# One PV run per eight score units throughout, ten score buffers to the end, and a VectorE write between the two halves of a bank

## The chip, the cores and the metric

One of the eight cores of a Trainium2 chip runs the kernel. The metric is the device time of one execution in microseconds; the median of three runs counts.

## The reference

`x` is 2048 x 512. A 32-head attention (head width 16) and a gated feed-forward block are computed from the same `x` and mixed per row by a sigmoid gate. All is float32.

```
qkv = x @ wqkv;  scores = q k^T / 4;  p = softmax(scores);  a = concat(p v) @ wo
b = (silu(x @ w1) * (x @ w3)) @ w2          # w1, w3: 512 x 1792, w2: 1792 x 512
g = sigmoid(sum(x * gate_w));  out = g * a + (1 - g) * b
```

## The kernel before

**Head of the program.** `x` is transposed and split into a rounded high part and a rest. The first Q and K columns and all of V are projected. Then one long main stretch begins, and a short ending follows it.

**The main stretch** is written out by hand as a string of letters, `order`, that is walked once. TensorE executes its instructions in that order.

- `Q` is one *score unit* (`score`, matmul in L719, exponential in L723). For one head pair, 128 keys and 512 queries, two matmuls of 50 rows each run side by side in the two row halves of the array and fill one `S` tile (`psum2()`, two tiles in all). ScalarE's exponential of 128 x 1024 turns the tile into one score buffer `p0` to `p9`. There are 1024 units, 32 for each head pair and half of the queries.
- `P` stands for two units' PV products (`pv`, L706). Four matmuls write four column groups of the accumulator `acc`. After 32 units `evac` copies `acc` out on VectorE (L687) and stores it.
- `F` is one *work slot* (`feed`). Everything else is cut into 158 *blocks*, each an accumulation of 12 or 42 matmuls into one of three banks (`bank()`): the remaining Q and K projections and the gate and up products (L409), the down products (L518), and the first output products (L597). The upper 64 rows of the array run a whole block first; then the lower 64 rows run the same block with the other half of the contraction into the same bank. Upper and lower half work on different blocks side by side, one matmul each per slot. After the lower half, the block's `done` function takes the bank off on VectorE.

`state_f` holds the two blocks in work. `REST` is the number of slots between the end of a block and the reuse of its bank. `GAP` is how many score units must lie between the end of an upper half and the start of the lower half of the same block. Nothing else than the order on TensorE stands between the two halves.

`order` has two kinds of period, each with eight units:

```
one = "QFFF" * 7 + "QPPPP"
two = ["QFFF" * 5 + "QPPQQPP", "QFFF" * 6 + "PPQQPP"]
order = "QQFFF" + one * LONG + "".join(two[...] for i in range(short))
order += "QFFF" * 4 + "QPPQPP"
```

`LONG` is 83 and `short` 44; with `MID` = 0 only the first entry of `two` is used. At the last Q ahead of a P, the exponentials of the SiLU that are due (L437, list `soon`) are issued behind the unit's own. VectorE's small pieces of work (`small`: reciprocals in L440, the addition in L438, products in L458) are issued one or two at each Q, and so are loads and the stages of the softmax division (`divide`, `reciprocals`).

In the first 83 periods all ten score buffers are used. Later only eight come back (`if n < 8 or issued < WIDE`); `p8` and `p9` then hold two rows of blocks of `wo` (`load_wo`) and a pair of tiles in `divide`.

**The ending** finishes the last blocks (`while feed(0, 0)`), divides the last heads, and projects and mixes the last rows.

Of the kernel before, what the change touches and what calls it, by code (L numbers as in the profile page):

```python
# [8 lines left out]
F32 = mybir.dt.float32  # L9
F32R = mybir.dt.float32r  # L10
# [7 lines left out]
P = 128  # L18
S = 2048
D = 512  # L20
F = 1792
# [6 lines left out]
NPAIR = H // 2  # L28
# [5 lines left out]
def gated_mix_kernel(ctx: ExitStack, tc: tile.TileContext, x, wqkv, wo, w1, w3, w2, gate_w, out):  # L34
# [18 lines left out]
    nc = tc.nc  # L53
# [3 lines left out]
    const = ctx.enter_context(tc.tile_pool(name="const", bufs=1))  # L57
# [23 lines left out]
    def slot(tag, dtype=F32R, shape=(P, 512)):  # L81

        return (fw if tag[0] == "f" else fk).tile(list(shape), dtype, name=tag, bufs=BUFS.get(tag, 2))
# [4 lines left out]
    def bank():  # L88
        return psum.tile([P, 512], F32, name="f", bufs=3)
# [21 lines left out]
    xn, xH, xL = {}, {}, {}  # L111
# [282 lines left out]
    wk = ctx.enter_context(tc.tile_pool(name="wk", bufs=1))  # L394
# [10 lines left out]
    def w_product(chunk, which, b):  # L405
        def product(ps, r, n):
            w = chunk["w"][which]
            k, i = divmod(n, 3)
            nc.tensor.matmul(ps, w[i == 2][r, k, :], (xL if i == 1 else xH)[b][r, k, :],  # L409
                             start=n == 0 and r.start == 0, stop=n == 3 * ND - 1 and r.start > 0)  # L410
        return product

# [67 lines left out]
    w2H, w2L, hs, wo_, ot = [], [], {}, {}, {}  # L480
    SETS = (("raw", "raw", "raw", "gw", "fh1", "fl1", "fh3", "fl3"), ("fh1", "fl1", "fh3", "fl3", "fr", "fr", "fr", "hx"))

    def halves_of(src, hi, lo, tag):

        r = slot(tag, F32)
        n = hi.shape[-1]
        nc.sync.dma_start(r[:, 0:n] if len(src.shape) == 2 else r[:, 0:n].rearrange("p (f t) -> p f t", t=P), src)
        nc.gpsimd.tensor_copy(hi, r[:, 0:n])  # L488
        nc.gpsimd.tensor_sub(lo, r[:, 0:n], hi)  # L489
# [7 lines left out]
    def load_piece(t, q):  # L497
        hi, lo = (slot(SETS[t % 2][2 * q + i]) for i in range(2))
        tag = "fr" if t == 0 or t == 1 and q < 2 else "sg"
        n = min(4, NF - 4 * q)  # L500
        src = h_d[512 * q:512 * q + P * n, P * t:P * t + P].rearrange("(f p) t -> p f t", p=P)
        halves_of(src, hi[:, 0:P * n], lo[:, 0:P * n], tag)
        hs.setdefault(t, []).append((hi, lo))

    def load_wo(k):
        if k < 2:
            hi, lo = w2H[3][:, 2 + k, :], w2L[3][:, 2 + k, :]
        else:
            both = wk.tile([P, 2, 512], F32R, name=f"p{NP - k + 1}")
            hi, lo = both[:, 0, :], both[:, 1, :]  # L510
        halves_of(wo[P * k:P * k + P, :], hi, lo, "sg")
        wo_[k] = hi, lo

    def h_product(t):
        def product(ps, r, n):
            f, i = divmod(n, 3)
            q, o = divmod(f, 4)
            nc.tensor.matmul(ps, hs[t][q][i == 2][r, P * o:P * o + P], (w2L if i == 1 else w2H)[q][r, o, :],  # L518
                             start=n == 0 and r.start == 0, stop=n == 3 * NF - 1 and r.start > 0)
            if r.start and i == 2 and (o == 3 or f == NF - 1):  # L520
                if t + 2 < NT:
                    load_piece(t + 2, q)
                elif t == NT - 2:
                    load_ot(q)
                elif q < 2:
                    load_ot(4 + q)
        return product

    def h_done(t):
# [11 lines left out]
    def load_ot(t):  # L541
        n = (0, 1, 2, 3, 2, 3, 0, 1)[t]
        hi, lo = (slot(SETS[0][2 * n + i]) for i in range(2))
        halves_of(N_d[:, P * t:P * t + P].rearrange("(k p) t -> p k t", p=P), hi[:], lo[:], "fr" if t >= 4 else "sg")
        ot[t] = hi, lo
# [3 lines left out]
    def reciprocals(k, half):  # L549

        rows = lambda d: d[8 * k:8 * k + 8, 1024 * half:1024 * half + 1024].rearrange("h (a t) -> h a t", a=16)
        nc.sync.dma_start(dd, rows(D_d))
        for _ in range(5):
            yield
        nc.vector.reciprocal(dd, dd)
        yield
        nc.sync.dma_start(rows(R_d), dd)

    def fetch_o(k, b, o, r, e=nc.sync):
        e.dma_start(o, O_d[P * k:P * k + P, 512 * b:512 * b + 512])  # L560
        src = R_d[8 * k:8 * k + 8, 512 * b:512 * b + 512]
        nc.sync.dma_start(r, bass.AP(tensor=src.tensor, offset=src.offset, ap=[[S, 8], [0, DH], [1, 512]]))

    def divide(k, half):

        yield from reciprocals(k, half)
        for b in (2 * half, 2 * half + 1):
            for _ in range(5):
                yield
            if half == 0:  # L570
                o, r = slot("hx", F32), slot("gw", F32)
            else:
                both = wk.tile([P, 2, 512], F32, name=f"p{NP - 1}")
                o, r = both[:, 0, :], both[:, 1, :]
            fetch_o(k, b, o, r)
            for _ in range(7):
                yield
            nc.gpsimd.tensor_mul(o, o, r)
            for _ in range(3):
                yield  # L580
            nc.sync.dma_start(N_d[P * k:P * k + P, 512 * b:512 * b + 512], o)
            yield
        if (k, half) == (2, 1):
            load_wo(2)
# [3 lines left out]
    def load_bt(t, tag="gs"):  # L588
        bt[t] = slot(tag, F32)
        nc.sync.dma_start(bt[t], B_d[P * t:P * t + P, :])  # L590

    def o_product(t):
        def product(ps, r, n):
            if n == 0 and r.start:
                load_bt(t)
            k, i = divmod(n, 3)
            nc.tensor.matmul(ps, ot[t][i == 2][r, P * k:P * k + P], wo_[k][i == 1][r, :],  # L597
                             start=n == 0 and r.start == 0, stop=n == 3 * ND - 1 and r.start > 0)
        return product

# [47 lines left out]
    source = blocks()  # L648

    ready, state_f = [], dict(upper=None, lower=None, started=0, ended=0)  # L650
    REST, GAP = 7, 3
    left_at = []

    def feed(rest=REST, gap=GAP):

        st = state_f
        used = st["started"] - 3
        if st["upper"] is None and (used < 0 or used < st["ended"] and left_at[used] + rest <= clock):
            block = next(source, None)
            if block:  # L660
                st["upper"] = [*block, bank(), 0]
                st["started"] += 1
        if st["lower"] is None and ready and ready[0][0] + gap <= issued:
            st["lower"] = ready.pop(0)[1]
        did = 0
        for name, r in (("upper", slice(0, 64)), ("lower", slice(64, P))):
            t = st[name]
            if t is None:
                continue
            product, done, length, ps, n = t  # L670
            did += 1
            product(ps, r, n)
            t[4] = n + 1
            if n + 1 == length:
                st[name] = None
                if name == "upper":
                    t[4] = 0
                    ready.append((issued, t))
                else:
                    done(ps)  # L680
                    st["ended"] += 1
                    left_at.append(clock)
        return did
# [18 lines left out]
    def pv(two):  # L702
        for j, half, k, gq, n, p in two:
            for h in range(2):
                r = 32 * (2 * gq + h)
                nc.tensor.matmul(acc[r:r + DH + 1, :], V[:, k, 2 * j + h, :], p[:, h, :],  # L706
                                 start=k == 0, stop=k == NT - 1)
            if n < 8 or issued < WIDE:
                free.append(n)
        if k == NT - 1:  # L710
            evac(j, half)

# [15 lines left out]


    NP = 10  # L730
    PERIODS = 8 * NPAIR
    LONG, MID = 83, 0
    WIDE = 8 * LONG
    one = "QFFF" * 7 + "QPPPP"
    two = ["QFFF" * 5 + "QPPQQPP", "QFFF" * 6 + "PPQQPP"]
    short = PERIODS - 1 - LONG
    order = "QQFFF" + one * LONG + "".join(two[(i + 1) * MID // short > i * MID // short] for i in range(short))
    order += "QFFF" * 4 + "QPPQPP"
    free = list(range(NP))

    units = iter([(j, half, k, gq) for half in range(2) for j in range(NPAIR) for k in range(NT) for gq in range(2)])
    pend, issued, clock = [], 0, 0
# [26 lines left out]
            pend = pend[2:]  # L769
    assert not pend and issued == 64 * NPAIR  # L770

    assert state_f["upper"] is None and all(b[0] < issued for b in ready)
    for _ in reciprocals(ND - 1, 1):
        pass
    k = ND - 1
    orr = [(slot("fr", F32), slot("sg", F32)) for _ in range(2)]
    for b in (2, 3):
        fetch_o(k, b, *orr[b - 2], nc.scalar)
    while feed(0, 0):
        pass  # L780
    assert state_f["ended"] == NBLOCK and not small and not later and not stages and not soon and not loads


    for t in (NT // 2 - 2, NT // 2 - 1):
        ps = bank()
# [4 lines left out]
    for t in range(NT // 2, NT):  # L790
        n, r = divmod(t - NT // 2, 2)
        if n < 2:
            if r == 0:
                both = psum2()
# [17 lines left out]
    for b in (2, 3):  # L812
        o, r = orr[b - 2]
# [34 lines left out]
```

## Time and profile before

| | |
|---|---|
| runs | 1418.3, 1418.87, 1421.13 us; median 1418.87 |
| profiled execution: span (the only time that the page has of it) | 1417.6 us |
| TensorE matmul / weight load busy | 1408.8 us (99%) / 833.7 us (59%) |
| ScalarE busy | 1033.2 us (73%) |
| VectorE / GpSimd busy | 449.4 us (32%) / 321.1 us (23%) |
| DMA | 141.42 MB, mean 100 GB/s |

The page has the engines' busy shares, the span in 40 slices, the DMA queues, the chain of work that ended last, and the costliest groups of instructions (line, engine, tiles, count, busy time, mean of one, idle time ahead of it and what ended that). A timeline row has its start, its length, the instruction and, in brackets, the idle time before it with what ended it; `x2` means that two instructions in a row are merged. PE is TensorE, ACT ScalarE, DVE VectorE, POOL GpSimd, SP the engine that issues most DMAs.

### The profile page before, as it was taken

To read this page: it belongs to the slowest core of one execution; us is meant where nothing else is said; L and a number is where in the kernel's file an instruction comes from. 1 tells how busy PE (TensorE), PEld (TensorE's weight loads), DVE (VectorE), ACT (ScalarE), POOL (GpSimd) and SP (SyncE) were. 2 spreads that over 40 slices of the span, in tenths; PEclk is the share of its full clock that TensorE was granted. 3 is DMA by queue.
4 is the path that set the end of the run, shared out by engine and by line. 5 is a ranking of instruction groups with operands and counts; after the bars stand their busy time and mean duration, and the time that the engine had idled before them with its cause. 6 is when DMAs were issued, how large, how long until landed. Compare 5 with 4: busy or idle time off the path is not lost.

```text
span 1417.6 us, 28518 instructions
## 1 busy us (share of the span) xinstructions
PE 1408.8 (99%) x11399; PEld 833.7 (59%) x11399; DVE 449.4 (32%) x845; ACT 1033.2 (73%) x1153; POOL 321.1 (23%) x356
## 2 busy tenths in 40 slices
PE   9999999999999999999999999999999999999998
PEld 7865656656556566565565665655555555554556
DVE  4421102464555545455464545400000000000013
ACT  4556767777777777777777777777788778877870
POOL 5014443011011100110110015441332332233230
PEclk9999999999999999999999999999999999999999
DMA  7554455342124432223233234543534443345445
GB/s 197 141 121 114 126 140 128 73 110 69 46 61 85 113 69 61 70 72 87 68 76 79 76 81 122 136 101 74 126 81 102 104 105 70 66 112 106 106 133 182
DMA packets 112668, 141.42 MB, mean 100 GB/s; under 512 B 16400, under 2 KB 70672, under 8 KB 109456
## 3 DMA queue, kind: packets, MB, share of 16 engines
q1 hardware_dynamic: 110384, 135.72, 39.6%
q10 hardware_dynamic: 2144, 3.80, 0.8%
q8 instruction: 92, 1.51, 0.5%
q14 instruction: 48, 0.39, 0.1%
HBM read 90.70 MB, written 48.76 MB: 98 GB/s over the span
## 4 chain that ended last, share of the span: by engine, by line
PE 93%; POOL 0%; DMA 0%; DVE 0%; ACT 0%; issue 0%; SPq 0%; ACTq 0%; POOLq 0%
PE acc L706 32%; PE f L409 27%; PE S L719 19%; PE f L518 11%; PE f L597 1%; PE f L95 0%; PE f L97 0%; PE f L96 0%; DMA fr<-in_B_w_dram 0%; PE S L97 0%; PE S L96 0%; PE S L95 0%; POOL xL L489 0%; POOL fl L489 0%; DVE sg L458 0%; POOL xH L488 0%
## 5 line engine op out<-in xcount | busy, mean ns | idle before, releaser
L723 ACT ACTIVATE p<-S 128x1024 f32<-128x1024 f32 x1024 | 967.5, 1026 | 308.4 <-PE S L719 307.1
L706 PE MATMUL acc<-p,V 128*17 128x512 f32 x4096 | 473.5, 594 | 0.0
L719 PE MATMUL S<-Qt,Kt 50*128 50x512 f32 x2048 | 427.9, 413 | 1.1 <-POOLq L278 0.6
L719 PEld LDWEIGHTS S<-Qt,Kt 50*128 50x128 f32 x2048 | 193.8, 184 | 187.4 <-ACT p L723 80.4
L706 PEld LDWEIGHTS acc<-p,V 128*17 128x17 f32 x4096 | 102.8, 97 | 274.1 <-issue 273.9
L409 PE MATMUL f<-xL,fh 64*128 64x512 f32 x1024 | 205.1, 391 | 0.0
L409 PE MATMUL f<-xH,fl 64*128 64x512 f32 x1024 | 204.9, 390 | 0.0
L409 PE MATMUL f<-xH,fh 64*128 64x512 f32 x1024 | 204.7, 390 | 0.0
L440 DVE RECIPROCAL sg<-sg 128x64 f32<-128x64 f32 x448 | 201.2, 509 | 1.9
L409 PEld LDWEIGHTS f<-xL,fh 64*128 64x128 f32 x1024 | 99.4, 187 | 21.2
L409 PEld LDWEIGHTS f<-xH,fl 64*128 64x128 f32 x1024 | 98.5, 185 | 20.1
L409 PEld LDWEIGHTS f<-xH,fh 64*128 64x128 f32 x1024 | 99.4, 187 | 17.7
L321 POOL CAST fh<-fr 128x512 fp32r<-128x512 f32 x32 | 21.6, 674 | 371.1 <-DMA fr<-in_B_w_dram 246.5
L687 DVE COPY u<-acc 128x512 f32<-128x512 f32 x32 | 22.1, 692 | 257.0 <-PE acc L706 257.0
L518 PE MATMUL f<-xH,fl 64*128 64x512 f32 x224 | 82.2, 391 | 0.5 <-POOL fl L489 0.5
L518 PE MATMUL f<-xL,fh 64*128 64x512 f32 x224 | 82.2, 391 | 0.3 <-POOL xL L489 0.3
L518 PE MATMUL f<-xH,fh 64*128 64x512 f32 x224 | 82.1, 391 | 0.0
L518 PE MATMUL f<-xH,raw 64*128 64x512 f32 x192 | 74.9, 390 | 0.0
L532 DVE TENSOR_SCALAR gs<-f,omg 128x512 f32<-128x512 f32 x16 | 12.0, 751 | 176.4 <-PE f L518 176.4
L432 DVE COPY gs<-f 128x512 f32<-128x512 f32 x56 | 38.7, 691 | 78.1 <-PE f L409 78.1
L518 PE MATMUL f<-xH,fr 64*128 64x512 f32 x160 | 62.4, 390 | 0.0
L454 DVE TENSOR_TENSOR raw<-f,gs 128x512 f32<-128x512 f32 x50 | 34.1, 682 | 82.7 <-PE f L409 82.7
(216 smaller groups left out, 1309.6 us busy)
## 6 DMA issues: line engine op xcount, KB each, us to landing
Kt<-kH_d SPq DMA_DIRECT2D x128, 128.0 KB
h_d<-sg SPq DMA_DIRECT2D x56, 256.0 KB
sg<-h_d SPq DMA_DIRECT2D x43, 256.0 KB
fr<-in_B_w_dram SPq DMA_DIRECT2D x42, 256.0 KB
Qt<-qH_d SPq DMA_DIRECT2D x128, 64.0 KB
Kt<-kL_d SPq DMA_DIRECT2D x64, 128.0 KB
fr<-in_A_wqkv_dram SPq DMA_DIRECT2D x18, 256.0 KB
Qt<-qL_d SPq DMA_DIRECT2D x64, 64.0 KB
```

What stands on the lines that cost most here:

```text
L321: nc.gpsimd.tensor_copy(wh, r)
L409: nc.tensor.matmul(ps, w[i == 2][r, k, :], (xL if i == 1 else xH)[b][r, k, :], start=n == 0 and r.start == 0, stop=n == 3 * ND - 1 and r.s ...
L432: nc.vector.tensor_copy(gs, ps)
L440: small.append(lambda q=q: nc.vector.reciprocal(sg[:, q:q + 64], sg[:, q:q + 64]))
L454: nc.vector.tensor_mul(gu, ps, st["gs"])
L518: nc.tensor.matmul(ps, hs[t][q][i == 2][r, P * o:P * o + P], (w2L if i == 1 else w2H)[q][r, o, :], start=n == 0 and r.start == 0, stop=n = ...
L532: nc.vector.tensor_scalar(y, ps, omg[:, t:t + 1], None, op0=OP.mult)
L597: nc.tensor.matmul(ps, ot[t][i == 2][r, P * k:P * k + P], wo_[k][i == 1][r, :], start=n == 0 and r.start == 0, stop=n == 3 * ND - 1 and r. ...
L687: nc.vector.tensor_copy(u, acc)
L706: nc.tensor.matmul(acc[r:r + DH + 1, :], V[:, k, 2 * j + h, :], p[:, h, :], start=k == 0, stop=k == NT - 1)
L719: nc.tensor.matmul(ps[:, h, :], Kt[i][r:r + 50, P * k:P * k + P], Qt[i][r:r + 50, t:t + 512], start=True, stop=True)
L723: nc.scalar.activation(p, ps, AF.Exp, scale=SCALE)
```

## The change

All periods become alike: two units, then the work slots, then units spread among slots, and one PV run of eight units. The work slots, 2403 over 127 periods, are shared out evenly (18 or 19 in each); the string's head and tail stay. All ten score buffers stay in use, and the two parts of `wo` and the tiles of `divide` get tiles of their own; the scratch for dynamic DMA descriptors is made smaller, which gives the room. When an upper half ends, VectorE writes one element (`tick`) after its last matmul, and the first matmul of the lower half waits for that write. `REST` and `GAP` are 9 and 6 and both count slots; a lower half may start earlier where no upper half is in work.

```diff
-            both = wk.tile([P, 2, 512], F32R, name=f"p{NP - k + 1}")
+            both = wk.tile([P, 2, 512], F32R, name=f"wo{k}")
...
-                both = wk.tile([P, 2, 512], F32, name=f"p{NP - 1}")
+                both = wk.tile([P, 2, 512], F32, name="od")
...
-    REST, GAP = 7, 3
+    REST, GAP = 9, 6
+    tick = const.tile([1, 1], F32, name="tick")
+    def after(ins, earlier):
+        tc.add_manual_dep(ins.ins, earlier.ins.name, ...)
...
-        if st["lower"] is None and ready and ready[0][0] + gap <= issued:
+        if st["lower"] is None and ready and (ready[0][0] + gap <= clock or st["upper"] is None):
...
-            product(ps, r, n)
+            ins = product(ps, r, n)
+            if turn and n == 0:
+                after(ins, turn)
...
-                    t[4] = 0
-                    ready.append((issued, t))
+                    t[4], t[5] = 0, nc.vector.memset(tick, 0.0)
+                    after(t[5], ins)
+                    ready.append((clock, t))
...
-            if n < 8 or issued < WIDE:
-                free.append(n)
+            free.append(n)
...
-    PERIODS = 8 * NPAIR
-    LONG, MID = 83, 0
-    WIDE = 8 * LONG
-    one = "QFFF" * 7 + "QPPPP"
-    two = ["QFFF" * 5 + "QPPQQPP", "QFFF" * 6 + "PPQQPP"]
-    ...
+    PERIODS = 8 * NPAIR - 1
+    PRODUCTS = 2403
+    def period(n):
+        return "QQ" + "F" * (n - 14) + "QFFF" * 4 + "QFFQPPPP"
+    share = [(i + 1) * PRODUCTS // PERIODS - i * PRODUCTS // PERIODS for i in range(PERIODS)]
+    order = "QQFFF" + "".join(period(n) for n in share) + "QFFF" * 4 + "QPPQPP"
...
-    while feed(0, 0):
-        pass
+    while feed(0):
+        clock += 1
...
-    nc = _bacc.Bacc("TRN2", target_bir_lowering=False, num_devices=1)
+    nc = _bacc.Bacc("TRN2", target_bir_lowering=False, num_devices=1, dynamic_dma_scratch_size=1024)
```

More of the change, by code (lines that the diff above doesn't have):

```diff
@@ L408, in product @@
             k, i = divmod(n, 3)
-            nc.tensor.matmul(ps, w[i == 2][r, k, :], (xL if i == 1 else xH)[b][r, k, :],
+            return nc.tensor.matmul(ps, w[i == 2][r, k, :], (xL if i == 1 else xH)[b][r, k, :],
                              start=n == 0 and r.start == 0, stop=n == 3 * ND - 1 and r.start > 0)
@@ L517, in product @@
             q, o = divmod(f, 4)
-            nc.tensor.matmul(ps, hs[t][q][i == 2][r, P * o:P * o + P], (w2L if i == 1 else w2H)[q][r, o, :],
+            ins = nc.tensor.matmul(ps, hs[t][q][i == 2][r, P * o:P * o + P], (w2L if i == 1 else w2H)[q][r, o, :],
                              start=n == 0 and r.start == 0, stop=n == 3 * NF - 1 and r.start > 0)
@@ L526, in product @@
                     load_ot(4 + q)
+            return ins
         return product
@@ L596, in product @@
             k, i = divmod(n, 3)
-            nc.tensor.matmul(ps, ot[t][i == 2][r, P * k:P * k + P], wo_[k][i == 1][r, :],
+            return nc.tensor.matmul(ps, ot[t][i == 2][r, P * k:P * k + P], wo_[k][i == 1][r, :],
                              start=n == 0 and r.start == 0, stop=n == 3 * ND - 1 and r.start > 0)
@@ L650, in gated_mix_kernel @@
     ready, state_f = [], dict(upper=None, lower=None, started=0, ended=0)
-    REST, GAP = 7, 3
+    REST, GAP = 9, 6
+    tick = const.tile([1, 1], F32, name="tick")
     left_at = []
+    def after(ins, earlier):
+        tc.add_manual_dep(ins.ins, earlier.ins.name,
+                          mybir.DependencyInfo(mybir.DependencyClass.Sync, mybir.DependencyReason.DATA),
+                          reason="the two halves of the array write a bank in turn")
     def feed(rest=REST, gap=GAP):
@@ L660, in feed @@
             if block:
-                st["upper"] = [*block, bank(), 0]
+                st["upper"] = [*block, bank(), 0, None]
                 st["started"] += 1
-        if st["lower"] is None and ready and ready[0][0] + gap <= issued:
+        if st["lower"] is None and ready and (ready[0][0] + gap <= clock or st["upper"] is None):
             st["lower"] = ready.pop(0)[1]
@@ L669, in feed @@
                 continue
-            product, done, length, ps, n = t
+            product, done, length, ps, n, turn = t
             did += 1
-            product(ps, r, n)
+            ins = product(ps, r, n)
+            if turn and n == 0:
+                after(ins, turn)
             t[4] = n + 1
@@ L730, in gated_mix_kernel @@
     NP = 10
-    PERIODS = 8 * NPAIR
-    LONG, MID = 83, 0
-    WIDE = 8 * LONG
-    one = "QFFF" * 7 + "QPPPP"
-    two = ["QFFF" * 5 + "QPPQQPP", "QFFF" * 6 + "PPQQPP"]
-    short = PERIODS - 1 - LONG
-    order = "QQFFF" + one * LONG + "".join(two[(i + 1) * MID // short > i * MID // short] for i in range(short))
-    order += "QFFF" * 4 + "QPPQPP"
+    PERIODS = 8 * NPAIR - 1
[4 more added lines that the diff above has]
+    order = "QQFFF" + "".join(period(n) for n in share) + "QFFF" * 4 + "QPPQPP"
     free = list(range(NP))
@@ L770, in gated_mix_kernel @@
     assert not pend and issued == 64 * NPAIR
-    assert state_f["upper"] is None and all(b[0] < issued for b in ready)
+    assert state_f["upper"] is None
     for _ in reciprocals(ND - 1, 1):
```

## The prediction

> **What bounds the kernel now.** First the page: its busy shares, the granted clock and the chain that ended last. Then the two costliest groups.
>
> ```profile
> span 1417.6 us, 28518 instructions
> PE 1408.8 (99%) x11399; PEld 833.7 (59%) x11399; DVE 449.4 (32%) x845; ACT 1033.2 (73%) x1153; POOL 321.1 (23%) x356
> PEclk9999999999999999999999999999999999999999
> PE 93%; POOL 0%; DMA 0%; DVE 0%; ACT 0%; issue 0%; SPq 0%; ACTq 0%; POOLq 0%
> L723 ACT ACTIVATE p<-S 128x1024 f32<-128x1024 f32 x1024 | 967.5, 1026 | 308.4 <-PE S L719 307.1
> L706 PE MATMUL acc<-p,V 128*17 128x512 f32 x4096 | 473.5, 594 | 0.0
> ```
>
> TensorE bounds the span: 93% of the last chain, full clock, busy 99%. ScalarE's 1024 exponentials leave it idle for 308.4 us, all waiting for scores. That is an average. What decides this change is the order inside one period of eight score units, so I read the timeline there. A period of the first kind (one PV run per eight units, 21 work slots):
>
> ```profile
> 503.21 0.40 PE L719 MATMUL S<-Qt,Kt 50*128 50x512 f32 x2
> 503.54 3.63 PE L706 MATMUL acc<-p,V 128*17 128x512 f32 x32
> 507.10 0.50 PE L719 MATMUL S<-Qt,Kt 50*128 50x512 f32 x2
> 507.44 0.40 PE L409 MATMUL f<-xH,fh 64*128 64x512 f32 x2
> 507.67 0.40 PE L409 MATMUL f<-xL,fh 64*128 64x512 f32 x2
> 507.90 0.40 PE L409 MATMUL f<-xH,fl 64*128 64x512 f32 x2
> ...
> 513.70 0.41 PE L719 MATMUL S<-Qt,Kt 50*128 50x512 f32 x2
> 514.03 3.63 PE L706 MATMUL acc<-p,V 128*17 128x512 f32 x32
> 507.70 7.53 ACT L723 ACTIVATE p<-S 128x1024 f32<-128x1024 f32 x8 [2.96 <-PE S L719]
> 515.13 0.62 ACT L437 ACTIVATE sg<-gs 128x512 f32<-128x512 f32 x1
> ```
>
> Call a score unit Q, a work slot F and two PV units P. Q and F take the same slot. From 507.44 to 513.70 there are 27 slots (21 F and 6 Q), so 6.26 / 27 = 0.232 us each. The first Q after a PV run is followed 0.34 us later instead of 0.23. From the last Q to the PV run is 0.33, and from the run's start to the next Q is 3.56. Sum: 0.34 + 27 x 0.232 + 0.33 + 3.56 = 10.49 us, which is 514.03 - 503.54. TensorE waits for nothing, and ScalarE idles 2.96 us per period.
>
> A period of the second kind (15 F, the PV run cut in two with two Q between):
>
> ```profile
> 1153.80 0.40 PE L719 MATMUL S<-Qt,Kt 50*128 50x512 f32 x2
> 1154.13 1.91 PE L706 MATMUL acc<-p,V 128*17 128x512 f32 x16
> 1155.97 0.73 PE L719 MATMUL S<-Qt,Kt 50*128 50x512 f32 x4
> 1156.63 1.91 PE L706 MATMUL acc<-p,V 128*17 128x512 f32 x16
> 1158.47 0.50 PE L719 MATMUL S<-Qt,Kt 50*128 50x512 f32 x2
> ...
> 1163.56 1.91 PE L706 MATMUL acc<-p,V 128*17 128x512 f32 x16
> 1156.60 1.94 ACT L723 ACTIVATE p<-S 128x1024 f32<-128x1024 f32 x2 [1.25 <-PE S L719]
> ```
>
> It takes 1163.56 - 1154.13 = 9.43 us. The middle of a span is 83 of the first kind and 44 of the second: 83 x 10.49 + 44 x 9.43 = 870.7 + 414.9 = 1285.6 us.
>
> **What is removed.** Afterwards all 127 periods have one run: Q Q, five F, four times Q F F F, then Q F F Q and four P. By the order strings, 2403 F over 127 periods make 117 periods of 19 F and 10 of 18; the total of Q, F and P is the same as before. With nothing waiting, a period of 19 F is 0.34 + 25 x 0.232 + 0.33 + 3.56 = 10.03 us, one of 18 F 9.80. That is 117 x 10.03 + 10 x 9.80 = 1271.5 us: 14.1 us less, the price of 44 extra PV runs (0.32 each).
>
> **What is added: a wait of the scores for ScalarE.** A Q writes one of two S tiles, so unit n needs exponential n-2 to be done. Before, Qs stand 0.93 us apart. Afterwards the first two come together and the last only three slots after the one before it. ScalarE's speed under load is read from the program's start, where it is saturated, and the rule of the wait from two places where a score really waited:
>
> ```profile
> 87.12 1.02 ACT L723 ACTIVATE p<-S 128x1024 f32<-128x1024 f32 x1
> 91.64 2.00 ACT L723 ACTIVATE p<-S 128x1024 f32<-128x1024 f32 x2
> 519.41 1.03 ACT L723 ACTIVATE p<-S 128x1024 f32<-128x1024 f32 x1 [0.20 <-ACT p L723]
> 520.26 0.40 PE L409 MATMUL f<-xH,fl 64*128 64x512 f32 x2
> 520.50 0.49 PE L719 MATMUL S<-Qt,Kt 50*128 50x512 f32 x2
> 520.83 0.39 PE L409 MATMUL f<-xH,fh 64*128 64x512 f32 x2
> 1055.46 1.03 ACT L723 ACTIVATE p<-S 128x1024 f32<-128x1024 f32 x1 [0.85 <-PE S L719]
> 1056.31 0.40 PE L518 MATMUL f<-xH,gw 64*128 64x512 f32 x1
> 1056.87 0.39 PE L518 MATMUL f<-xH,raw 64*128 64x512 f32 x1
> ```
>
> The exponentials that start at 87.12 and 91.64 are five steps apart: 0.904 us each. The step from the first to the second after an idle stretch is 1.94 - 1.02 = 0.92. At 519.41 the exponential ends at 520.44; the Q was due at 520.26 + 0.232 = 520.49, 0.05 later; the F behind it came 0.57 after the F before instead of 0.464, so 0.11 was lost. At 1055.46: end 1056.49, due 1056.54, again 0.05, lost 0.56 - 0.464 = 0.10. So a Q loses what its due time is short of the exponential's end plus 0.16.
>
> Count a period from its first Q. Exponential 0 starts at 0.60 (507.70 - 507.10) and ends at 1.62; exponential 1 starts at 1.52, later ones 0.904 apart, so exponential 5 starts at 5.14 and ends at 6.16. Q2 is due at 0.34 + 6 x 0.232 = 1.73 and may go at 1.78: 0.05 lost. Q3 to Q6 then come 0.93 apart, 0.01 to 0.08 after their bounds (Q3 due 2.71, bound 1.52 + 1.02 + 0.16 = 2.70), and lose nothing. Q7 is due at 1.78 + 16 x 0.232 + 0.70 = 6.19 and may go at 6.32: 0.13 lost. The period is 6.32 + 0.33 + 3.56 = 10.21 us, for 18 F too, since the same exponential sets it. I take 10.22. If every step took the 0.92 of the first, Q7 would go at 0.60 + 5 x 0.92 + 1.02 + 0.16 = 6.38 and the period be 10.27; with no wait it is 10.03. 127 x 10.22 = 1297.9: **12.3 us more** than before. The balance lies at 1285.6 / 127 = 10.12.
>
> [...]
>
> The gate exponentials (L437, 0.62 us) stay hidden. They are issued behind the last Q; exponential 7 ends near 8.0, one or two more by 9.2, and the next exponential starts at 10.8. Without the PV run above them each would cost its 0.62.
>
> About one exponential in 64 starts 0.2 to 0.3 us late without visible reason (519.41, idle 0.20, and 1055.46 are two of 15). Before, slack left 0.10 of it. Afterwards six of eight places pass it on whole: 16 x 6/8 x 0.28 = 3.4, less some 1.6 paid already. I take 1, bounds 0 and 3.
>
> **What is added: the tick.** There are 158 blocks, each with one 1x1 VectorE write, and the first matmul of the lower half waits for it. Behind that matmul in TensorE's queue stand all later Q, F and P; ScalarE then waits for the Qs. Rows:
>
> ```profile
> 507.23 0.69 DVE L687 COPY u<-acc 128x512 f32<-128x512 f32 x1 [4.32 <-PE acc L706]
> 508.35 0.69 DVE L432 COPY gs<-f 128x512 f32<-128x512 f32 x1 [0.42 <-PE f L409]
> 516.25 1.79 DVE L440 RECIPROCAL sg<-sg 128x64 f32<-128x64 f32 x4
> L234 DVE TENSOR_SCALAR flag<-top 1x1 int32<-1x1 f32 x1 | 0.1, 141 | 0.0
> L330 DVE MEMSET acc<- 128x512 f32 x1 | 0.5, 485 | 0.9 <-PEq L834 0.9
> DVE sg L438 <- ACT sg L437: 103.0, 56, 4.0
> ```
>
> The matmul at 507.90 ends at 508.30 and the copy starts 0.05 later. A tick is no 128x512 memset (0.485) but like the 1x1 operation (0.14): it is done 0.40 + 0.05 + 0.14 = 0.59 after the upper half's last matmul starts. Counted in the order, 115 lower halves start 6 to 8 slots after that, 1.39 us at least, and 43 start 24 or more after it. A weight load runs about one slot ahead, so some 0.57 us is spare. One copy of 0.69 ahead of the tick would cost 0.12. Worst is a tick soon after a period's accumulator copy: the copy ends 0.82 after the first Q, three reciprocals (0.45 each) at 2.17, and the two or three such blocks lose 0.2 to 0.4. L438's waits for ScalarE (up to 4.0) fall under PV runs, where no tick stands. Bounds: 0, and 115 x 0.12 = 14 if a copy always stood ahead; I take 1, nearest to the idle row.
>
> **The rest at nothing.** Own tiles for two output weights and the late products replace two shared score tiles; their loads are issued at the same units and nothing in the chain waits there. Two more score buffers in the second kind gain nothing by themselves: ScalarE's idle time there is a wait for scores (1156.60, idle 1.25), not for a buffer. The smaller descriptor scratch only makes room. The span's end drains 4 F slots instead of 6: 2 x 0.23 = 0.5 less. At the hand-over to the last product TensorE waits on a weight load in one period; it moves but stays.
>
> Sum: 12.3 + 1 + 1 - 0.5 = +13.8. The profiled execution has 1417.6; the runs' median lies 1.27 above it, which I keep: 1418.87 + 13.8 = **1433 us**.
>
> **Rivals.**
> - *Faster: the wait is not there.* If exponentials under load stepped 0.88 us or less, or scores found their tile sooner, the period would tend to 10.03 and only the removed switches would count: 1418.9 - 14.1 + 1.5 = 1406. Decisive point: a period below 10.12. For: ScalarE is busy only 73%. Against: 0.904 and both measured losses. 0.10.
> - *About equal: half the wait.* A period of 10.12 gives 1419 to 1420. It needs Q2 and Q7 together to lose 0.09 instead of 0.18. 0.06.
> - *The tick binds.* If half of the 115 close blocks found a copy and a reciprocal ahead (0.12 + 0.45), 33 us would be added, some of it hidden in the wait of Q7: about 1450. For: VectorE is an in-order queue with copies that wait. Against: 32% busy. 0.10.
> - *Slow exponentials.* At 0.94 per step Q7 goes at 0.60 + 5 x 0.94 + 1.18 = 6.48 and the period is 10.37: 19 us more, 1452. For: a first step out of idle takes 0.92. Against: the saturated row's 0.904. 0.04. [...]
>
> **Numbers.** Forecast 0.70, with 1424 to 1443 of its own (period 10.16 to 10.28, ticks 0 to 5). The range for 8 in 10 takes in part of the tick rival and the equal case: 1418 to 1446. Faster by over 0.2% (2.8 us, about what a measurement can tell) 0.10, within it 0.07, slower 0.83.
>
> **What would show it.** Right: PV runs start 10.2 us apart throughout; in a period's timeline the last Q stands 0.1 to 0.2 late against three slots, and eight exponentials run without idle time; TensorE's weight loads of S wait for ScalarE in nearly every period; the first lower-half matmuls wait for VectorE for under 5 us in all. Wrong: a period of 10.03 (no wait), waits for the tick above 10 us, or a changed span before the first or after the last PV run.

## The result and the profile after

The change makes the kernel slower: 1445.28 us (median of four runs, 1444.22 to 1446.49) against 1419.14 us (four runs beside them). The ratio is 1.0176, 95% interval 1.0157 to 1.0195. The prediction was 1433 us with a range of 1418 to 1446: the direction is right, the size is not. Forecast were 13.8 us more, measured 26.1. The time lies outside the 1424 to 1443 us that the forecast itself allowed, and inside the range by less than 1 us.

One thing is needed to read the numbers: some executions of both kernels lose 2 to 5 us (one of them 8) to a halved granted clock near the start of the main stretch (the dip, below), by their mean clocks (0.998 or less instead of 0.999 or 1.000) all four of the changed kernel and 19 of the 47 of the kernel before that were run beside the experiments.

First the page of the changed kernel: its span, busy shares, granted clock, and the groups of the exponentials and the ticks (busy time and mean ns of one, then the idle time ahead and what ended it). The last line is from the list of waits: the weight loads of the scores, which waited for an exponential (us in all, times, longest).

```profile
span 1444.7 us, 28752 instructions
PE 1431.3 (99%) x11399; PEld 821.4 (57%) x11399; DVE 460.6 (32%) x1003; ACT 1019.7 (71%) x1153; POOL 319.0 (22%) x356
PEclk9989999999999999999999999999999999999999
L731 ACT ACTIVATE p<-S 128x1024 f32<-128x1024 f32 x1024 | 954.6, 1049 | 349.3 <-PE S L727 348.2
L685 DVE MEMSET tick<- 1x1 f32 x158 | 9.3, 59 | 365.5 <-PE f L518 198.7
PEld S L727 <- ACT p L731: 81.6, 325, 0.9
```

TensorE looks as busy as before, 99%, though it has lost 27 us. Its busy time has grown by 22.5 us for the same 11399 matmuls: the mean record of a score's matmul has grown from 413 to 430 ns, and at the hand-over, at a clock of 0.50, a block's matmul takes 0.62 us instead of 0.39, all of it counted as busy, so the busy share does not show this loss. The mean exponential has grown from 1026 to 1049 ns. The weight loads of the scores waited for an exponential 325 times, against 106 times before (81.6 and 80.4 us in all). What shows the loss is the order in one period. The timeline of one period of the changed kernel, PV runs and scores of TensorE, then ScalarE:

```profile
560.61 3.63 PE L715 MATMUL acc<-p,V 128*17 128x512 f32 x32
564.17 0.73 PE L727 MATMUL S<-Qt,Kt 50*128 50x512 f32 x4
565.89 0.46 PE L727 MATMUL S<-Qt,Kt 50*128 50x512 f32 x2
...
569.68 0.39 PE L727 MATMUL S<-Qt,Kt 50*128 50x512 f32 x2
570.43 0.49 PE L727 MATMUL S<-Qt,Kt 50*128 50x512 f32 x2
570.85 3.63 PE L715 MATMUL acc<-p,V 128*17 128x512 f32 x32
564.77 7.44 ACT L731 ACTIVATE p<-S 128x1024 f32<-128x1024 f32 x8 [2.31 <-PE S L727]
564.77 1.03 ACT L731 ACTIVATE p<-S 128x1024 f32<-128x1024 f32 x1 [2.31 <-PE S L727]
569.30 1.07 ACT L731 ACTIVATE p<-S 128x1024 f32<-128x1024 f32 x1
```

The period is 570.85 - 560.61 = 10.24 us. Eight exponentials run without idle time between them, as forecast. The last Q starts at 570.43, three slots and 0.05 us after the one before, and the PV run follows it by 0.42 instead of 0.33: the marks of a Q that waited. Exponential 5 ends at 569.30 + 1.07 = 570.37. The prediction's rule then lets the PV run start at 570.37 + 0.16 + 0.33 = 570.86; it starts at 570.85.

One period is different. The intervals between PV runs are 10.24 to 10.27 us in nearly all the span and 10.38 to 10.55 in ten of them, but one is 16.16 and the next 10.99. That is the hand-over, where the work passes from the gate and up products to the down products. The timeline there, then the wait of TensorE for a tick, two pieces of the chain, and the start of two PV runs at the same place in the kernel before:

```profile
961.03 3.63 PE L715 MATMUL acc<-p,V 128*17 128x512 f32 x32
968.58 0.62 SPq L553 DMA_DIRECT2D dd<-d_d  x1
972.42 0.55 DVE L556 RECIPROCAL dd<-dd 128x64 f32<-128x64 f32 x1 [6.12 <-DMA dd<-d_d]
972.90 0.69 DVE L454 TENSOR_TENSOR hx<-f,gs 128x512 f32<-128x512 f32 x1
972.92 0.06 DVE L685 MEMSET tick<- 1x1 f32 x1
977.19 4.36 PE L715 MATMUL acc<-p,V 128*17 128x512 f32 x32
```
```profile
PE f L409 <- DVE tick L685: 3.6, 1, 3.6
```
```profile
963.13 5.43 DMA Kt<-kH_d
...
968.58 3.82 DMA dd<-d_d
```
```profile
913.35 0.62 PE L706 MATMUL acc<-p,V 128*17 128x512 f32 x4
925.16 0.62 PE L706 MATMUL acc<-p,V 128*17 128x512 f32 x4
```

The tick stands in VectorE's queue behind a product (L454), and that stands behind the reciprocal of the softmax division (L556), which waits for its load `dd`. In the chain this load is issued only when a load of `Kt` is through. So the lower half of a block waited 3.6 us for a division that it has nothing to do with, and all Qs and PV runs stood behind it. The granted clock then falls. Windows of 2 us there (busy time of PE, PEld, DVE, ACT, POOL; then granted clock, DMA share and GB/s):

```profile
970.00:972.00 2.00, 0.00 (x0) 0.00 (x0) 0.00 (x0) 0.01 (x1) 0.00 (x0) 0.97 0.83 227
972.00:974.00 2.00, 0.94 (x4) 0.83 (x6) 1.17 (x3) 0.00 (x0) 1.59 (x2) 0.50 0.48 136
974.00:976.00 2.00, 2.00 (x12) 1.55 (x10) 0.00 (x0) 1.02 (x1) 1.92 (x3) 0.50 0.23 52
```

TensorE stood still for 3.6 us, and the clock was 0.50 from 971.9 to 978.7. The last matmul ended at 969.4, so the clock fell after 2.5 us of idle time.

The third place is the opening. Windows of the changed kernel, with the first PV run of it and of the kernel before (L706):

```profile
84.00:88.00 4.00, 2.26 (x12) 1.22 (x10) 1.03 (x2) 1.23 (x2) 1.27 (x1) 0.98 0.23 57
88.00:92.00 4.00, 3.88 (x13) 2.70 (x14) 0.00 (x0) 2.89 (x4) 0.00 (x0) 0.50 0.79 154
92.00:96.00 4.00, 4.00 (x16) 3.14 (x14) 0.06 (x1) 2.63 (x3) 0.00 (x0) 0.50 0.80 98
99.00 1.05 PE L715 MATMUL acc<-p,V 128*17 128x512 f32 x8
```
```profile
88.00:92.00 4.00, 4.00 (x23) 2.96 (x24) 0.00 (x0) 4.00 (x6) 0.00 (x0) 1.00 0.76 160
94.18 2.34 PE L706 MATMUL acc<-p,V 128*17 128x512 f32 x20
```

From 87.8 to 98.1 the changed kernel has clock 0.50, the profiled execution of the kernel before 1.00. This is the dip. The longest idle stretch of TensorE just ahead of it is 1.2 us.

The account of the two spans, 1444.7 - 1417.6 = 27.1 us:

| part | us |
|---|---|
| first PV run later (99.00 instead of 94.18) | +4.8 |
| hand-over: 16.16 + 10.99 - 2 x 10.25 = 6.6, against 1.3 before (one interval of 11.81 instead of 10.49) | +5.3 |
| all other periods, with the late exponentials | +17.4 |
| after the start of the last PV run (35.17 instead of 35.58) | -0.4 |

The third line is the rest of the sum; 127 x 10.25 - 1285.6 = 16.1 explains nearly all of it. The first is nearly all clock: the profiled execution of the old order (below) has the same dip, and its first PV run starts at 99.17.

### The profile page after: what moved, and what is told of

Same layout as the page of the kernel before. It is cut to its first block, busy times and chain, and to the rows that moved or that the text cites. A ratio compares the mean times of both kernels' runs of the same rounds, so it can differ in the third digit from the quotient of the medians.

```text
span 1444.7 us, 28752 instructions
## 1 busy us (share of the span) xinstructions
PE 1431.3 (99%) x11399; PEld 821.4 (57%) x11399; DVE 460.6 (32%) x1003; ACT 1019.7 (71%) x1153; POOL 319.0 (22%) x356
## 4 chain that ended last, share of the span: by engine, by line
PE 92%; ACT 1%; DMA 1%; issue 0%; SPq 0%; DVE 0%; ACTq 0%; DVEq 0%
PE acc L715 31%; PE f L409 26%; PE S L727 20%; PE f L518 11%; PE f L598 1%; ACT p L731 1%; DMA Kt<-kH_d 0%; PE f L95 0%; PE f L97 0%; PE f L96 0%; DMA dd<-d_d 0%; PE S L97 0%; PE S L96 0%; PE S L95 0%; SPq L261 0%
## 5 line engine op out<-in xcount | busy, mean ns | idle before, releaser
L731 ACT ACTIVATE p<-S 128x1024 f32<-128x1024 f32 x1024 | 954.6, 1049 | 349.3 <-PE S L727 348.2
L715 PE MATMUL acc<-p,V 128*17 128x512 f32 x4096 | 465.6, 594 | 0.0
L409 PE MATMUL f<-xH,fh 64*128 64x512 f32 x1024 | 348.7, 393 | 3.6 <-DVE tick L685 3.6
L409 PE MATMUL f<-xL,fh 64*128 64x512 f32 x1024 | 350.0, 393 | 0.0
L409 PE MATMUL f<-xH,fl 64*128 64x512 f32 x1024 | 349.6, 393 | 0.0
L409 PEld LDWEIGHTS f<-xH,fh 64*128 64x128 f32 x1024 | 190.8, 186 | 19.9 <-DVE tick L685 4.1
L409 PEld LDWEIGHTS f<-xL,fh 64*128 64x128 f32 x1024 | 190.7, 186 | 16.5
L409 PEld LDWEIGHTS f<-xH,fl 64*128 64x128 f32 x1024 | 190.9, 186 | 15.6
L685 DVE MEMSET tick<- 1x1 f32 x158 | 9.3, 59 | 365.5 <-PE f L518 198.7
L518 PE MATMUL f<-xH,fl 64*128 64x512 f32 x224 | 87.1, 392 | 0.0
L518 PE MATMUL f<-xL,fh 64*128 64x512 f32 x224 | 87.1, 392 | 0.0
L518 PE MATMUL f<-xH,fh 64*128 64x512 f32 x224 | 87.1, 392 | 0.0
L438 DVE TENSOR_SCALAR sg<-sg 128x512 f32<-128x512 f32 x56 | 29.7, 530 | 122.3 <-ACT sg L437 122.3
```

Of the source, the lines that this page charges most:

```text
L409: return nc.tensor.matmul(ps, w[i == 2][r, k, :], (xL if i == 1 else xH)[b][r, k, :], start=n == 0 and r.start == 0, stop=n == 3 * ND - 1 ...
L438: small.append(lambda: nc.vector.tensor_scalar(sg, sg, 1.0, None, op0=OP.add))
L518: ins = nc.tensor.matmul(ps, hs[t][q][i == 2][r, P * o:P * o + P], (w2L if i == 1 else w2H)[q][r, o, :], start=n == 0 and r.start == 0, st ...
L685: t[4], t[5] = 0, nc.vector.memset(tick, 0.0)
L731: nc.scalar.activation(p, ps, AF.Exp, scale=SCALE)
```

## The experiments

The theory was: the steady loss is the wait of the last Q for exponential 5, the loss at the hand-over is a tick behind a load, and the loss in the opening is the clock. The rivals: the ticks cost something everywhere, or the other parts of the change (buffers, tiles, scratch) do. The line numbers are those of the changed kernel.

**The old order in the changed kernel.** All else stays: ticks, ten buffers, own tiles.

```diff
+    one = "QFFF" * 7 + "QPPPP"
+    two = "QFFF" * 5 + "QPPQQPP"
...
-    order = "QQFFF" + "".join(period(n) for n in share) + "QFFF" * 4 + "QPPQPP"
+    order = "QQFFF" + one * 83 + two * 44 + "QFFF" * 4 + "QPPQPP"
```

> The changed kernel with one part undone: the order string of before (83 periods of 21 work slots and one PV run, 44 periods of 15 and two runs). Ten buffers, own tiles, the tick and REST and GAP of the change stay; 108 of the 158 lower halves now start 6 slots after their upper half. Theory A (the even order makes the scores wait for the exponentials; the tick itself costs next to nothing): periods 10.49 and 9.43 as before, 1418 to 1423 us. Theory B (the tick lengthens the periods, about 0.1 us for each of the 158 blocks): 1435 us or more with the old order too. Theory C (the second buffer set or the smaller descriptor scratch slows the loads): also well above 1423.

Measured: 1418.47 us (median of ten), ratio to the kernel before 0.9987 (0.9972 to 1.0002). Its timeline, one period of each kind:

```profile
509.16 3.63 PE L715 MATMUL acc<-p,V 128*17 128x512 f32 x32
519.67 3.63 PE L715 MATMUL acc<-p,V 128*17 128x512 f32 x32
...
1151.53 1.91 PE L715 MATMUL acc<-p,V 128*17 128x512 f32 x16
1160.96 1.91 PE L715 MATMUL acc<-p,V 128*17 128x512 f32 x16
```

The periods are 10.51 and 9.43, as in the kernel before (10.49 and 9.43). TensorE has no wait for a tick at all. So ticks, buffers and tiles by themselves cost nothing that can be measured, and the whole loss comes with the order.

**A shorter exponential in the even order.** The exponential covers 384 of the 512 queries; the rest of each score buffer is a constant 1.

```diff
-        p = wk.tile([P, 2, 512], F32, name=f"p{n}")
-        nc.scalar.activation(p, ps, AF.Exp, scale=SCALE)
+        p = fixed[n]
+        nc.scalar.activation(p[:, :, 0:384], ps[:, :, 0:384], AF.Exp, scale=SCALE)
...
+    fixed = [wk.tile([P, 2, 512], F32, name=f"p{n}") for n in range(NP)]
+    for t in fixed:
+        nc.gpsimd.memset(t, 1.0)
```

> The changed kernel with exponentials of 384 instead of 512 queries per head (a quarter of them is left out, the rest of each score buffer holds ones). Everything else stays: order, tick, PV. Theory A: a step of ScalarE falls from 0.904 to about 0.7 us, no score waits, periods go from 10.25 to 10.03 (19 slots): 127 x 0.22 = 28 us less, 1415 to 1420 us. Theory B (tick, or slots that are slower in the even order): periods stay at 10.25 and the time near 1445.

Measured: 1416.53 us (one run). Its timeline:

```profile
600.43 3.63 PE L715 MATMUL acc<-p,V 128*17 128x512 f32 x32
609.45 0.40 PE L727 MATMUL S<-Qt,Kt 50*128 50x512 f32 x2
610.16 0.40 PE L727 MATMUL S<-Qt,Kt 50*128 50x512 f32 x2
610.49 3.63 PE L715 MATMUL acc<-p,V 128*17 128x512 f32 x32
604.59 6.89 ACT L731 ACTIVATE p<-S 128x768 f32<-128x768 f32 x8 [2.65 <-PE S L727]
```

The last two Qs are 0.71 apart, three slots, and the PV run follows by 0.33: nothing waits. The period is 10.06 here and 10.02 to 10.06 in most others (9.88 with 18 F), close to the prediction's sum for an order without a wait (10.03 and 9.80). The wait on ScalarE is therefore the steady loss, 0.21 us per period or 27 us in all, of which the removed switches give some 12 back. This run still had the hand-over stall (a wait of 3.7 us for a tick, an interval of 15.79) and, by its mean clock of 0.995, the halved clock in the opening. Without those two, some 5 us each, the 1416.5 us would by this estimate be near 1406, the time of the rival without a wait.

**Uneven work.** Periods with 22 and with 15 or 16 F in turn, the same number in all.

```diff
-    share = [(i + 1) * PRODUCTS // PERIODS - i * PRODUCTS // PERIODS for i in range(PERIODS)]
+    share = [22 if i % 2 == 0 else 16 - (i % 10 == 1) for i in range(PERIODS)]
+    share[-1] += PRODUCTS - sum(share)
...
```

> The changed kernel with the same 2403 work slots shared unevenly: 64 periods of 22 and 63 of 15 or 16, each with one PV run and the same two, then spread, score units. Theory A: a period of 22 slots costs its slots, 0.34 + 28 x 0.232 + 3.89 = 10.73 us, and one of 15 or 16 still 10.25, because six exponentials in a row set it: 64 x 10.73 + 63 x 10.25 = 1332 against 1302 us, some 31 us more, about 1476. Theory B (cost per slot, per run or per tick): the sum of slots is the same, so the time is too, 1445.

Measured: 1480.59 us (one run). Three PV runs of its timeline:

```profile
699.78 3.63 PE L715 MATMUL acc<-p,V 128*17 128x512 f32 x32
710.56 3.63 PE L715 MATMUL acc<-p,V 128*17 128x512 f32 x32
720.80 3.63 PE L715 MATMUL acc<-p,V 128*17 128x512 f32 x32
```

10.78 and 10.24 in turn. A period with 15 or 16 F takes as long as one with 18 or 19: the F taken out give nothing back, since exponential 5 sets the time. A period with 22 F pays for its slots: 10.73 by the prediction's sum without a wait. Here the waits are long enough to show as idle time: the profile has 65 of TensorE's scores waiting for an exponential, 35.9 us in all. Where this wait holds, work put into it is free and work taken out gains nothing: 10.24 with 15 or 16 F as with 18 or 19.

**A fat tick.** The write is 128x512 instead of 1x1.

```diff
-    tick = const.tile([1, 1], F32, name="tick")
+    tick = const.tile([P, 512], F32, name="tick")
```

> The changed kernel with the tick made long: a write of 128 x 512 elements (0.485 us in the trace of before) instead of one element (0.06 us). Theory A: an upper half ends at least 1.39 us before its lower half starts, so a write 0.43 us longer still fits; periods stay at 10.25, 1444 to 1449 us. Theory B (the lower halves wait for the tick): 115 close blocks x 0.43 = up to 49 us more.

Measured: 1446.21 us (one run). The group of the ticks, two PV runs and the only wait on a tick:

```profile
L685 DVE MEMSET tick<- 128x512 f32 x158 | 76.6, 485 | 436.5 <-PE f L409 200.2 <-PE f L518 180.8 <-PE f L598 19.9
600.74 3.63 PE L715 MATMUL acc<-p,V 128*17 128x512 f32 x32
610.99 1.48 PE L715 MATMUL acc<-p,V 128*17 128x512 f32 x12
PE f L409 <- DVE tick L685: 4.1, 1, 4.1
```

Each tick takes eight times as long, 485 ns instead of 59, and the period stays 10.25. So the steady loss does not depend on the length of a tick. Only the wait at the hand-over grows, from 3.6 to 4.1, about the 0.43 by which one tick became longer.

**The division later.** One stage of the softmax division starts at unit 716 instead of 680, so that its reciprocal is not queued on VectorE at the hand-over.

```diff
-            if issued % 128 == (40 if issued // 128 == 5 else 12) and 1 <= issued // 128 < 8:
+            if issued % 128 == (76 if issued // 128 == 5 else 12) and 1 <= issued // 128 < 8:
```

> The changed kernel with one stage of the softmax division moved from unit 680 to unit 716, so that its reciprocal, which waits for a load, no longer stands in VectorE's queue ahead of the tick at the hand-over to the down products. Theory A2 (the 16.15 us period there is this tick, 3.63 us, and the halved clock behind it): that period falls to 10.3 to 11.8 and the one after to 10.25, 5 to 6.5 us less, 1438 to 1441. Theory D (TensorE would have waited there anyway for the first weights of the down products, which land on GpSimd at the same time): at most 2 us less.

Measured: 1439.43 us (four runs), ratio 1.0145 (1.0129 to 1.0161) to 1419.35. The hand-over in its timeline:

```profile
958.96 3.63 PE L715 MATMUL acc<-p,V 128*17 128x512 f32 x32
969.34 3.63 PE L715 MATMUL acc<-p,V 128*17 128x512 f32 x32
979.60 3.63 PE L715 MATMUL acc<-p,V 128*17 128x512 f32 x32
```

The intervals are 10.38 and 10.26 instead of 16.16 and 10.99, 6.5 us less, and the median is 5.9 us below that of the changed kernel, both with the dip. So the loss there was the reciprocal ahead of the tick, with the halved clock behind it.

**The opening.** Three kernels keep TensorE busier in the opening with spare transposes, four ahead of the row maxima and three after the first three F: in the changed kernel alone, with the later division, and with the old order.

```diff
+    idle(4)
...
+            if i == 4:
+                idle(3)
```

> The changed kernel with seven small transposes into the unused accumulator in TensorE's idle places at the opening of the main stretch: four ahead of the branch, three behind the first three work slots. Theory E (the granted clock of 0.50 over some 8 us there follows from TensorE's idle time): it stays at 1.00, the first PV run starts near 94.2 instead of 98 to 100 us, and the time is 4 to 5 us less wherever the dip had been, about 1441. Rival (the dip comes from the time at which the stretch starts, not from idle time): the dip stays in part of the runs.

> The changed kernel with both: the stage of the division at unit 716 and the seven transposes. If the two add up: 1434 to 1437 us. What is then left against before is the period: 127 x 10.25 = 1302 against 1286 us, 16 us, so a ratio near 1.011 to 1.012 to the runs of before that kept their clock.

> The changed kernel with the order string of before and the seven transposes. With the old order the time was 1418.5, in runs with and without the clock dip at the opening. Theory E: all runs near 1418, none near 1423. Against before, whose runs fall in both groups, 0 to 5 us less.

Measured: 1444.66 us with the transposes alone (four runs, 1441.98 to 1447.0), ratio 1.0173 (1.0154 to 1.0193): by their mean clocks the dip came in two of the four. With the later division 1435.83, ratio 1.0115 (1.0099 to 1.0130): three runs have a mean clock of 0.999 or 1.000 and take 1435.4 to 1436.1, one has 0.996 and takes 1441.0. In the old order 1418.67 (twelve runs), ratio 0.9996 (0.9981 to 1.0010), eight of them without the dip. So the dip costs about 5 us. In the even order the transposes make it rarer (3 of 8 executions, against all 8 of the changed kernel and of the one with the later division) and do not remove it; in the old order it comes in 4 of 12 with them and in 4 of 10 without.

The runs without the dip of the kernel with both are the cleanest measure of the period: 1435.4 to 1436.1 against 1418 to 1419.5 of the kernel before at full clock, 17 us more, where 127 x 10.25 - 1285.6 gives 16.1.

**The old opening in the even order**, with the later division: the first period keeps the old string's spread of its Qs.

```diff
-    order = "QQFFF" + "".join(period(n) for n in share) + "QFFF" * 4 + "QPPQPP"
+    order = "QQFFF" + "QFFF" * 6 + "QQPPPP" + "".join(period(n) for n in share[1:]) + "QFFF" * 4 + "QPPQPP"
```

> The changed kernel with the stage of the division at unit 716 and the first period in the shape of before (six times Q F F F, then Q Q and four P, 18 work slots). So far every run with the even opening and no added transposes had lost clock, and 13 of the 30 runs of before. Theory E (TensorE's idle waits in the even opening make the dip sure): with the old opening only about half of the runs have it, near 1439, and the others are at 1434 to 1435. Rival (the dip has nothing to do with the order): all runs have it, 1438 to 1441 as at unit 716 alone.

Measured: 1437.91 us (five runs), ratio 1.0123 (1.0105 to 1.0142). Four of five still have a dip, a smaller one (clock 0.998; the fifth takes 1435.6). The order of the first period may be a part of it but is not all. What decides between dip and no dip stays open: the same program does both.

**A mixed order.** Since one-run periods of 21 F wait for nothing, 89 of them and 38 shorter two-run periods of 14 or 15 F might beat the kernel before.

```diff
...
+    three_ = "QFFF" * 4 + "QFFQPPQQPP"
+    longs, shorts = 89, 38
+    order = "QQFFF" + one * longs + "".join(two if i in (12, 25) else three_ for i in range(shorts)) + "QFFF" * 4 + "QPPQPP"
```

> The rule that was found, used the other way: ten buffers, tick and own tiles, but 89 periods of 21 slots with one PV run and 38 of 14 or 15 with two. A period of 21 slots has no wait for the exponentials, one of 14 with two runs just has none (the sixth unit is due 4.52 us after the first, its bound is 4.52). Theory A: six runs fewer than with the old order: 89 x 10.51 + 38 x 9.20 = 1285.0 against 83 x 10.51 + 44 x 9.43 = 1287.2, 2 us less than the old order's 1418.5 in runs without the dip, 1416 to 1417. If the sixth unit waits after all, nothing is gained.

Measured: 1422.81 us (twelve runs), ratio 1.0018 (1.0006 to 1.0030): a miss. Its timeline in the second kind, and the wait at its hand-over:

```profile
1187.04 0.40 PE L727 MATMUL S<-Qt,Kt 50*128 50x512 f32 x2
1187.74 0.45 PE L727 MATMUL S<-Qt,Kt 50*128 50x512 f32 x2
1188.12 1.91 PE L715 MATMUL acc<-p,V 128*17 128x512 f32 x16
PE f L518 <- DVE tick L685: 2.0, 1, 2.0
```

The short period has its own wait: a Q 0.70 after the one before, then 0.38 instead of 0.33 to the PV run, and its two intervals sum to 9.25 where 9.20 was counted. And the order brought a tick behind the same reciprocal (L556), which waited for its load `dd`, once more: 2.0 us, with an interval of 13.03 instead of 10.51. The clock stayed at 1.00 there. No order that was tried beats the kernel before by a measurable amount. The even order without the tick was not tried.

## Why the prediction was right or wrong, point by point

The direction was right for the reason given: the wait of the scores outweighs the removed switches. The forecast was 12 us too low because three terms were too small or absent, all to the same side. That the time still lies in the range is in part luck: the range was widened upwards for another rival (ticks that bind throughout), and that rival did not come about.

- **Removed switches, -14.1.** Right within 2 us. With the wait gone (the shorter exponential, one run) the period is 10.04 in the mean of 10.02 and 10.06, forecast 10.03, and 9.88 with 18 F, forecast 9.80: 117 x 10.04 + 10 x 9.88 = 1273.5 instead of 1271.5.
- **The wait of the scores, net +12.3.** The mechanism was right, to the unit: Q7 behind exponential 5. The term was mis-sized: 10.25 instead of 10.22, 16.1 us instead of 12.3. The rule itself (end plus 0.16) held to 0.01. The step that failed is the one that put exponential 5's end at 5.56 after exponential 0's start, by one step of 0.92, four of 0.904 and a length of 1.02. It measures 570.37 - 564.77 = 5.60. The start of exponential 5 was right (4.54 forecast, 569.30 - 564.77 = 4.53 measured); its length was not. The 0.904 was read from start to start, but the recorded length grows along a burst, from 1.03 to 1.07 in the rows above. From end to end the prediction's own rows give (91.64 + 2.00 - 87.12 - 1.02) / 6 = 0.917, nearer to the 0.92 that was used only as an upper bound (10.27). A score waits for an end, so the ends had to be counted.
- **The rival of slow exponentials.** It did not come about: no run shows the 0.94 per step that it assumes. The bursts show 0.90 to 0.92 from start to start and 0.92 from end to end, and the period is 10.25, not 10.37.
- **Late exponentials, +1.** In agreement: ten periods of 10.38 to 10.55 instead of 10.25 add 2.3 in all, against a forecast 16 x 6/8 x 0.28 = 3.4 before what was already paid. The net was not separated from the rounding of the periods.
- **The tick, +1, bounds 0 to 14.** At the 115 close blocks right: no wait. The mean tick is 59 ns, less than the 141 assumed, and even 485 ns changed nothing. At the hand-over wrong: one wait of 3.6 us, and with the halved clock some 6. The step that failed is the list of what can stand ahead of a tick. It held copies, reciprocals of the gate and L438's waits for ScalarE, and left out L556, an operation that waits for a DMA in the same queue. The waits for `dd` were not looked up by their place in the order.
- **The hand-over "moves but stays".** Wrong for the reason just given: 6.6 instead of 1.3.
- **The clock.** The prediction has no term for it. The dip in the opening is worth about 5 us, and the profiled execution of the kernel before had none, so its page could not show it. Other executions of the kernel before do, by their mean clocks. Why the even order with its own opening had it in every execution without the transposes stays open.
- **The signs.** The eight exponentials without idle time, the last Q some 0.14 late (0.05 at its start, 0.09 more behind it), and a wait for ticks below 5 us came as named.
- **The end, -0.5; the rest at nothing.** Right: -0.4, and 1418.47 with the old order.

Of the 13.3 us by which the spans differ from the forecast (27.1 against 13.8), about 4 are the exponentials' ends, 4.3 the tick at the hand-over, where 1 was forecast, and 4.8 the opening.

## What to carry to other kernels

Even shares are worth nothing by themselves: a period with a wait in it gave nothing back for work taken out (10.24 us with 15 or 16 work slots as with 18 or 19), so spread the units that depend on a second engine before the bulk work is spread. When a wait is costed from a burst, count from end to end of the engine that releases (0.92 us here), not from start to start (0.904). Before a marker is put into an in-order queue, list everything in that queue that waits for a DMA (here L556, which cost TensorE 3.6 us), and look where it stands at each change of phase.

## What the runs showed of the hardware

- A 1x1 VectorE write took 59 ns in all 158 cases of the changed kernel. In the old order, where 108 of the 158 lower halves start six slots (1.4 us) after their upper half, TensorE showed no wait for it.
- A 1024-element exponential's recorded length grew from 1.03 to 1.10 us over eight in a row (from 564.77 on, the changed kernel), while starts stayed 0.90 to 0.92 apart.
- Around 3.6 us without a matmul the granted clock fell to 0.50 for 6.8 us (the hand-over of the changed kernel). At a wait of 2.0 us (the hand-over of the mixed order) it stayed at 1.00. In the opening of the changed kernel it fell to 0.50 with 2.26 of 4 us busy, and it stayed there for 10.2 us though TensorE was busy for 3.88 and 4.00 of the next 4 us each. By the mean clocks this happened in some executions and not in others of the same program: 0.996 in one execution of the kernel with both the later division and the transposes, 0.999 or 1.000 in its three others.
- The stretches at 0.50 last 10.24 us (opening) and 6.83 us (hand-over) in the changed kernel, and about 6.8 us in the opening with the later division: three, two and two times 3.41. Between the two stretches of the changed kernel lie 873.81 us, 256 times 3.413. So in that trace these changes of the clock stand whole multiples of 3.41 us apart.
